# Computing v of eight token tiles by seven half-width products a pair, with its weight sums on Pool

## The chip, the cores and the metric

The kernel runs on one core of a Trainium2 chip. The metric is device time in microseconds (us) of one execution, taken as the median of several runs. One execution is profiled by the hardware; its trace lists every instruction of the five engines: TensorE (PE, with its weight loads listed apart as PEld), VectorE (DVE), ScalarE (ACT), GpSimd (Pool) and SyncE (SP, which only issues DMAs here).

## The reference

All tensors are 32-bit floats. x has 2048 rows of 512; wqkv is 512x1536, wo 512x512, w1 512x1792, w2 1792x512.

```python
xn = layernorm(x)                          # no gain or bias, eps 1e-5
q, k, v = split(xn @ wqkv)                 # 32 heads of 16
idx = pos[:, None] - arange(8) * 2         # a window of 8 keys, every second row back
logits = einsum("bhsd,bhswd->bhsw", q, k[idx]) * 16 ** -0.5    # -1e9 where idx < 0
s = einsum("bhsw,bhswd->bhsd", softmax(logits), v[idx]) @ wo
h = square(relu(xn @ w1 + b1))
out = x + s * silu(h @ w2 + b2)
```

## The kernel before

**Tiles and precision.** Rows go in 16 tiles of 128 (NT), handled in pairs of tiles a and b = a + 1. A matrix product of 32-bit floats is made of three passes over a high and a low part of each operand, (high, high), (high, low), (low, high), called PASSES. `split` makes the two parts: ACT writes the high part, DVE or Pool subtracts it to get the low part.

**Two halves of the program.** The first half loads and normalises tiles, computes q, k and v, and writes them to DRAM (`sq`, `sk`, `sv`). The second half is the MLP over chunks of 512 rows: `up` (names `ph`, in two PSUM banks with tag `h`) and `down` (`pb`), for 14 blocks f of 128 columns, with the attention's output product `pw` among them. `up` of block f ends in ACT operations on its bank: relu in place, the square rounded to `h`, and for some f (of chunk 0, f below 2 and above 11) the full square to an SBUF tile `hf`, from which Pool makes the low part; for the others the square stays in the bank and DVE (`lowh`) reads it.

**Attention.** It runs on DVE in units u of 256 rows (one pair of tiles), `pr` and `pv` being its two large products with a reduction behind each. It loads k, q and v of a unit from DRAM by DMAs that ACT's queue issues (`load_u`). Its generator `attention` is advanced by `pump`, which compares modelled clocks of PE and DVE; `defer` and `flush` put loads and exponentials at modelled times.

**q, k and v of a pair.** An ordinary product (`qkv`) of one tile and one of q, k, v is 12 matmuls of 512 columns in a bank named `pq`. Pairs 4 to 14 (SEVEN) make q and k of both tiles by a scheme of seven products instead of eight, with 6 matmuls each (`product`, banks named `pm`): the operands are quarters of the normalised tiles (`xt`), sums of them (`S`, made on DVE from `Sf`), quarters of the weights (Q0, Q1, K0, K1) and sums of these (T1 to T4), all made beforehand. The products accumulate onto each other in three banks: `sums_ps` takes Q0, T2, T3 and T4 one after the other, and each running sum is evacuated by ACT before the next product adds to it. v of these pairs is made by two ordinary products among the seven.

**Staging.** Evacuations write to staging tiles (`stg`, four buffers for k, q and v of all pairs in turn), each of which is stored by one DMA that SP issues (`store_qkv`). A buffer is reused when its store has landed.

**Order.** All engines take instructions in program order. `plan`, filled by `at(a, step, ...)`, says what stands beside which of the six steps of a pair: the transposes and splits of tiles two ahead, the sums, and by `slots` the statistics (`stats` on DVE, `spread` on ACT for tiles from 8 on: a `mean` and a `var` operation whose elementwise result is not used), `norm` and `shuffle` (four DMAs on SP, then loads of later x). `ahead` places early splits of MLP weights. Every operation goes through the helper `Ordered`, so that all of them show line 87 in the profile of before, and DMAs of `queue` line 100.

Of the kernel before, what the change touches and what calls it, by code (L numbers as in the profile page):

```python
# [30 lines left out]
GR = 8  # L31
# [17 lines left out]

STATS = 8  # L50

MATMUL, TRANSPOSE, DVE_FIXED, SHARED, SLACK, LATE, ROOM0, ROOM = 227, 150, 150, 200, 500, 3000, 500, 3500

BEHIND, FREE, LAND, LOAD = 5000, 2000, 4500, 10500

# [2 lines left out]
def body(ctx: ExitStack, tc: tile.TileContext, x, wqkv, wo, w1, b1, w2, b2, out):  # L58
# [4 lines left out]

    def price(engine, name, a, k):
        if engine == "PE":
            return MATMUL if name == "matmul" else TRANSPOSE
# [47 lines left out]
    def psH(name):  # L114
        return psum.tile([P, 512], F32, name=name, tag="h", bufs=2)
# [129 lines left out]
    def attention():  # L245
# [91 lines left out]

                defer(max(clock["V"] + FREE if u else 0, done_tiles[n][1][u] + LAND), start)

        yield from load(0, "kqv")  # L340

        for u in range(NU + 1):
            if u < NU:
                Ls[u] = att.tile([P, BI * 4, W], F32, name=f"L{u}", tag="L", bufs=2)
                for s in range(4):
                    yield from qk(u, s)
                    if u == 0 and s % 2:
                        yield from soft_a(0, s // 2)
# [12 lines left out]
            if u:  # L361
                store(u - 1)
                if u < NU - 1:
                    yield from load(u, "v")
                if u < NU:
                    yield from soft_b(u)

    stream = attention()
    coming = [None]

# [162 lines left out]
    def part_s(a, j):  # L533
        return lambda p, i: Sp[a, j // 2][:, p, j % 2, i]

    def product(ps, lhs, w, start=True):

        k = 0
        for i in range(2):
            for p, q in PASSES:  # L540
                PE.matmul(ps, lhs(p, i), wq[w][:, q, i, :], start=start and k == 0, stop=k == 5,
                          skip_group_check=True)
                k += 1

    def heads(ps):
        return ps.rearrange("p (g c) -> p g c", g=GR)

    def new_stg(t, s):
        stgs[s] = pstg.tile([P, GR, 2, CH], F32, name=f"stg{t}_{s}", tag="stg", bufs=4)

    def qkv(t, s, between=None, late=False):
# [10 lines left out]
        evacuate(t, s, ps)  # L562

    def evacuate(t, s, ps):
        if t % 2 == 0:
# [119 lines left out]
    def split_sum(w, eng):  # L685
        for i in range(2):
            split(*sum_weights[w, i], eng)

    qkv(1, 2)
    for t in range(6, 10):  # L690
        load_x(t)
# [12 lines left out]
    for a in range(2, NT, 2):  # L704
# [7 lines left out]
        if seven:  # L712
# [5 lines left out]
            at(a, n + 2 if n else n + 4, low_sums, t, 0)  # L718
            at(a, n + 3 if n else n + 5, low_sums, t, 1)
    slots = {6: ((2, 2), (2, 2), (2, 2), (2, 3)), 8: ((2, 4), (2, 5), (4, 0), (4, 1)),  # L720
             10: ((4, 4), (4, 5), (6, 0), (6, 1)), 12: ((6, 2), (6, 3), (6, 4), (6, 5)),
             14: ((8, 1), (8, 2), (8, 4), (8, 5))}
    for t, places in slots.items():
        for i, (a, step) in enumerate(places):
# [2 lines left out]
                at(a, step, shuffle, t)  # L727
    for i, w in enumerate((T2, T3, T4)):
        at(2, 1 + i, split_sum, w, G)
    for i in range(2):  # L730
        at(4, i, load_w, i)

    ahead = {(10, 2): 1, (12, 4): 1, (14, 0): 1, (14, 2): 1, (14, 4): 1}

    def beside(a, step):

        for f, args in plan.get((a, step), ()):
            f(*args)
        for n in range(ahead.get((a, step), 0)):
            next_w()  # L740
        pump(LATE)

    def pair(a):
# [13 lines left out]
    def pair_of_seven(a):  # L757

        b, last = a + 1, a + 2 == NT
        new_stg(a, 1)  # L760
        new_stg(a, 0)
        q, k = stgs[0], stgs[1]
        sums_ps, first, five = (psA(f"pm{a}_{n}") for n in range(3))
        home = dict(pool=px, tag="x", bufs=4) if last else dict(pool=hpool, tag="hf")
        u2 = home.pop("pool").tile([P, GR, CH], F32, name=f"u2_{a}", **home)
# [10 lines left out]
        A.activation(q[:, :, 0], heads(first), AF.Copy)  # L776
        beside(a, 2)

        def seventh():
            product(sums_ps, part_s(a, 2), T3, False)  # L780
            A.activation(q[:, :, 1], heads(sums_ps), AF.Copy)
            G.tensor_add(k[:, :, 1], k[:, :, 1], q[:, :, 1])
            product(five, part_s(a, 3), K1, False)
            not_before(clock["PE"])
            V.tensor_add(k[:, :, 0], u2, heads(five))
            store_qkv(b, 1)
            beside(a, 3)

        if last:
            for f in range(2):  # L790
                up(0, f)
                pump()
            lowh(0)
        qkv(b, 2, seventh)
        beside(a, 4)
        product(sums_ps, part_x(b, 1), T4, False)
        A.activation(q[:, :, 1], heads(sums_ps), AF.Copy)
        store_qkv(b, 0)
        beside(a, 5)

# [211 lines left out]
```

## Time and profile before

| | |
|---|---|
| median of 3 runs | 488.46 us (488.23 to 488.54) |
| the profiled execution: its time | 488.73 us |
| its span | 486.8 us |
| PE busy | 478.8 us, 98% of the span |
| DVE busy | 417.6 us, 86% |
| ACT busy | 235.1 us, 48% |
| Pool busy | 204.1 us, 42% |
| pair 4 starts on PE | 41.78 us |
| pair 14 starts on PE | 119.56 us |

Times in the trace count from the start of the span. A row of a timeline has start, duration, engine, source line, operation, output from input, shape and count, and in brackets the idle time before it with what ended that idle time. Matmuls are pipelined: one lasts longer than the distance to the next, so their rate is read from starts.

### The profile page before, as it was taken

How to read it: one execution, taken by the hardware profiler on the slowest of the kernel's cores; microseconds unless marked ns; L12 is line 12 of the kernel's file. 1: busy time of each engine (PE TensorE's matmuls, PEld its weight loads, DVE VectorE, ACT ScalarE, POOL GpSimd, SP SyncE). 2: the span in 40 equal slices, each digit the busy share in tenths (PEclk: the TensorE clock that was granted, in tenths of full speed). 3: DMA queues.
4: the chain of work that ended last, by engine and by line, in shares of the span. 5: the costliest groups of instructions: out<-in, count | busy, mean ns of one | idle time of the engine just before them, and what ended most of it. 6: DMA issues, size and time to landing. Idle time of an engine off the chain costs nothing.

```text
span 486.8 us, 5931 instructions
## 1 busy us (share of the span) xinstructions
PE 478.8 (98%) x2118; PEld 393.8 (81%) x2118; DVE 417.6 (86%) x348; ACT 235.1 (48%) x421; POOL 204.1 (42%) x166
## 2 busy tenths in 40 slices
PE   8999999999999999999999999999999999999996
PEld 5888788886888888888888888888888888888885
DVE  5967968986869699999999999999989999959533
ACT  5548697645575576453422444343233543423240
POOL 1347232132756699235534332653524145353210
PEclk9999999999999999999999999999999999999999
DMA  7999999898757992943708184425723852330142
GB/s 278 248 247 275 308 303 260 200 277 276 218 160 197 254 226 91 254 130 68 193 18 200 53 227 139 102 86 125 182 72 71 270 125 86 82 102 27 49 138 76
DMA packets 71002, 81.47 MB, mean 167 GB/s; under 512 B 6204, under 2 KB 55612, under 8 KB 70972
## 3 DMA queue, kind: packets, MB, share of 16 engines
q1 hardware_dynamic: 65788, 54.87, 40.8%
q10 hardware_dynamic: 5184, 26.22, 22.1%
q8 instruction: 17, 0.28, 0.3%
q14 instruction: 13, 0.11, 0.1%
HBM read 50.60 MB, written 27.32 MB: 160 GB/s over the span
## 4 chain that ended last, share of the span: by engine, by line
PE 87%; DMA 5%; DVE 4%; ACT 2%; issue 1%; SPq 0%; POOL 0%; DVEq 0%; ACTq 0%; POOLq 0%
PE pb L87 31%; PE ph L87 31%; PE pq L87 10%; PE pw L87 9%; PE pm L87 5%; DMA sk<-stg 2%; DMA sx<-xt 1%; DVE L L87 1%; DMA xb<-xn 1%; DMA x<-in_A_x 1%; DVE pxT L87 1%; SPq L100 0%; ACT stg L87 0%; DVE pr L87 0%; ACT mean L87 0%
## 5 line engine op out<-in xcount | busy, mean ns | idle before, releaser
L87 PE MATMUL pb<-w,h 128*128 128x512 f32 x672 | 160.1, 389 | 0.0
L87 PEld LDWEIGHTS pb<-w,h 128*128 128x128 f32 x672 | 126.1, 188 | 26.2
L87 POOL TENSOR_TENSOR h<-hf,h 128x512 fp32r<-128x512 f32 x46 | 72.5, 1576 | 152.0 <-ACT hf L87 152.0
L87 PE MATMUL ph<-xU,w 128*128 128x512 f32 x504 | 120.2, 389 | 0.0
L87 ACT ACTIVATE ph<-ph,b1t 128x512 f32<-128x512 f32 x56 | 37.0, 661 | 161.4 <-PE ph L87 152.7
L87 PEld LDWEIGHTS ph<-xU,w 128*128 128x128 f32 x504 | 94.6, 188 | 19.6
L87 DVE TENSOR_TENSOR pr<-k,q 128x2048 f32<-128x2048 f32 x32 | 78.9, 2466 | 4.4 <-DMA q<-sq 3.9
L87 DVE TENSOR_TENSOR pv<-v,L 128x2048 f32<-128x2048 f32 x32 | 75.4, 2355 | 6.3 <-POOL L L87 5.5
L87 DVE TENSOR_REDUCE v<-pv 128x256 f32<-128x2048 f32 x32 | 73.0, 2281 | 0.8
L87 DVE TENSOR_REDUCE L<-pr 128x128 f32<-128x2048 f32 x32 | 72.9, 2279 | 0.7
L87 PE MATMUL pw<-wot,oT 128*128 128x512 f32 (+1 forms) x204 | 45.9, 376 | 0.0
L87 PEld LDWEIGHTS pw<-wot,oT 128*128 128x128 f32 x204 | 36.8, 188 | 7.1
L87 PE MATMUL ph<-xT,w 128*128 128x512 f32 x168 | 40.0, 389 | 0.0
L87 PE MATMUL pq<-wq,xt 128*128 128x512 f32 x144 | 36.0, 392 | 1.7 <-ACT stg L87 1.7
L87 PEld LDWEIGHTS ph<-xT,w 128*128 128x128 f32 x168 | 31.5, 188 | 6.5
L87 PE MATMUL pm<-wq,S 128*128 128x512 f32 x144 | 35.9, 391 | 0.1
L87 POOL TENSOR_TENSOR w<-w1r,w 128x512 fp32r<-128x512 f32 x14 | 22.4, 1598 | 29.1 <-ACT w L87 29.1
L87 ACT ACTIVATE h<-ph 128x512 fp32r<-128x512 f32 x56 | 33.7, 602 | 1.7
L87 PEld LDWEIGHTS pq<-wq,xt 128*128 128x128 f32 x144 | 26.8, 188 | 8.3 <-ACT stg L87 2.8
L87 PEld LDWEIGHTS pm<-wq,S 128*128 128x128 f32 x144 | 26.8, 188 | 6.4 <-ACT u L87 0.7
L87 PE MATMUL pq<-wq,xT 128*128 128x512 f32 x132 | 30.9, 393 | 0.0
L87 PEld LDWEIGHTS pq<-wq,xT 128*128 128x128 f32 x132 | 24.5, 188 | 5.8 <-ACT xT L87 0.7
(82 smaller groups left out, 486.8 us busy)
## 6 DMA issues: line engine op xcount, KB each, us to landing
k<-sk ACTq DMA_DIRECT2D x8, 960.0 KB, 7.4
v<-sv ACTq DMA_DIRECT2D x8, 960.0 KB, 7.5
sx<-xt SPq DMA_DIRECT2D x12, 512.0 KB, 5.7
xU<-sx ACTq DMA_DIRECT2D x12, 512.0 KB, 7.2
x<-in_A_x SPq DMA_DIRECT2D x16, 256.0 KB, 6.3
sk<-stg SPq DMA_DIRECT2D x8, 512.0 KB, 4.3
sq<-stg SPq DMA_DIRECT2D x8, 512.0 KB, 7.3
sv<-stg SPq DMA_DIRECT2D x8, 512.0 KB, 5.0
```

The source lines that it names most:

```text
L87: return tc.keep_in_program_order(f(*a, **k))
```

## The change

v of pairs 6, 8, 10 and 12 (tiles 6 to 13, VSEVEN) is made by the seven-product scheme as well, with products 256 columns wide, since the scheme is taken here between the two column halves of v's weight. Each v product stands behind the q or k product with the same left operand. Its banks are two of tag `h` (`pv_0`, `pv_2`) and one of the four others (`pv_1`). A pair's 24 matmuls of 512 columns become 42 of 256. ACT evacuates seven results of 256 columns instead of two of 512; Pool and DVE add one sum of 256 columns each.

The four weight sums of v are made by Pool from the raw weights (`sum_v`, beside steps 1 and 5 of pair 2) and split by ACT and Pool beside steps 0 to 3 of pair 4 (`split_v`, names `vsum`). The raw weights lie in the buffer of unit 0's v, so that unit's v load, which stood in pair 2, waits until step 3 of pair 4 has been written (`v_ready`) and until the attention has come to it.

In all pairs of SEVEN the staging tiles are taken in the order k, v, q, that of their stores; before, k and q were taken at the pair's start and v at its first evacuation. A temporary `u2` is gone: the sum goes into k's staging tile. `spread` writes its unused result to SBUF instead of the `h` banks. Tile 10's and 12's places in `slots` are one or more steps later, and two entries of `ahead` move.

```diff
+VSEVEN = range(6, 14, 2)
...
-MATMUL, TRANSPOSE, ... = 227, 150, ...
+MATMUL, VMATMUL, TRANSPOSE, ... = 227, 120, 150, ...
...
-        yield from load(0, "kqv")
+        yield from load(0, "kq")
...
+                    if u == 0 and s == 1:
+                        while not v_ready:
+                            yield None
+                        yield from load(0, "v")
...
-        A.activation(psH(f"mean{t}"), xins[t], AF.Copy, scale=-1.0 / D, accum_out=means[t])
-        A.activation(psH(f"var{t}"), xins[t], AF.Square, bias=means[t], accum_out=rs[t])
+        waste = hpool.tile([P, 512], F32, name=f"waste{t}", tag="hf")
+        A.activation(waste, xins[t], AF.Copy, scale=-1.0 / D, accum_out=means[t])
+        A.activation(waste, xins[t], AF.Square, bias=means[t], accum_out=rs[t])
...
+    def sum_v(n):
+        dst, a, b = (((0, vl), (0, vr), (0, vl)), ((2, vr), (2, vr), (0, vl)), ((0, vr), (2, vr), (0, vr)),
+                     ((2, vl), (2, vl), (2, vr)))[n]
+        dst, a, b = (raws[2][:, kt:kt + 2, cols] for kt, cols in (dst, a, b))
+        G.tensor_sub(dst, a, b)
+        v_sums[n] = dst
+
+    def split_v(n):
+        i = n // 2
+        if i not in v_parts:
+            v_parts[i] = buffer(f"vsum{i}", (10, K0)[i])
+        split(*(v_parts[i][:, q, :, (vl, vr)[n % 2]] for q in range(2)), v_sums[n], G)
...
-             10: ((4, 4), (4, 5), (6, 0), (6, 1)), 12: ((6, 2), (6, 3), (6, 4), (6, 5)),
+             10: ((4, 5), (6, 0), (6, 1), (6, 2)), 12: ((6, 3), (6, 4), (6, 5), (8, 0)),
...
+    for a, step, f, n in ((2, 1, sum_v, 0), (2, 1, sum_v, 2), (2, 5, sum_v, 1), (2, 5, sum_v, 3),
+                          (4, 0, split_v, 0), (4, 1, split_v, 1), (4, 2, split_v, 2), (4, 3, split_v, 3)):
+        at(a, step, f, n)
...
-    ahead = {(10, 2): 1, (12, 4): 1, (14, 0): 1, (14, 2): 1, (14, 4): 1}
+    ahead = {(12, 3): 1, (12, 5): 1, (14, 0): 1, (14, 2): 1, (14, 4): 1}
...
+        if (a, step) == (4, 3):
+            v_ready.append(True)
         pump(LATE)
...
-        new_stg(a, 1)
-        new_stg(a, 0)
-        q, k = stgs[0], stgs[1]
+        seven = a in VSEVEN
+        for s in (1, 2, 0):
+            new_stg(a, s)
+        q, k, v = (stgs[s] for s in range(3))
...
+        if seven:
+            v_first = psA(f"pv{a}_1")
+            v_sums_ps, v_five = psH(f"pv{a}_0"), psH(f"pv{a}_2")
         product(sums_ps, part_x(a, 0), Q0)
         A.activation(first, sums_ps, AF.Copy)
+        if seven:
+            first_v()
         product(five, part_s(a, 0), T1)
         A.activation(k[:, :, 1], heads(five), AF.Copy)
+        if seven:
+            product(v_five[:, vl], part_s(a, 0), v_parts[0], cols=vl)
+            A.activation(v[:, 4:, 1], heads(v_five[:, vl]), AF.Copy)
         beside(a, 0)
-        qkv(a, 2)
-        beside(a, 1)
+        if not seven:
+            qkv(a, 2, new=False)
+            beside(a, 1)
         product(sums_ps, part_s(a, 1), T2, False)
-        A.activation(u2, heads(sums_ps), AF.Copy)
+        A.activation(k[:, :, 0], heads(sums_ps), AF.Copy)
+        if seven:
+            product(v_sums_ps[:, vl], part_s(a, 1), v_parts[0], False, vr)
+            A.activation(v[:, 4:, 0], heads(v_sums_ps[:, vl]), AF.Copy)
+            beside(a, 1)
...
+        if seven:
+            sixth()
+            product(v_sums_ps[:, vl], part_s(a, 2), v_parts[1], False, vl)
+            A.activation(v[:, :4, 1], heads(v_sums_ps[:, vl]), AF.Copy)
+            G.tensor_add(v[:, 4:, 1], v[:, 4:, 1], v[:, :4, 1])
+            beside(a, 3)
+            seventh()
+            product(v_five[:, vl], part_s(a, 3), V1, False, vr)
+            not_before(clock["PE"])
+            V.tensor_add(v[:, 4:, 0], v[:, 4:, 0], heads(v_five[:, vl]))
...
         product(sums_ps, part_x(b, 1), T4, False)
         A.activation(q[:, :, 1], heads(sums_ps), AF.Copy)
+        if seven:
+            product(v_sums_ps[:, vl], part_x(b, 1), v_parts[1], False, vr)
+            A.activation(v[:, :4, 1], heads(v_sums_ps[:, vl]), AF.Copy)
+            store_qkv(b, 2)
         store_qkv(b, 0)
         beside(a, 5)
```

The order of instructions moves at three places. First, PE in pair 6, whole before, and after as far as the twelfth of its fourteen products (`pm` are products of q and k, `pq` and `pv` of v; `wq_111`, `wq_112`, `wq_114`, `wq_117` to `wq_120` are the weight parts Q0, Q1, K1, T1 to T4, and `vsum` the sums of v). Before:

```order
L87 MATMUL pm_0_727<-wq_111,xt_611 128x512 x6
L87 MATMUL pm_2_729<-wq_117,S_0_678 128x512 x6
L87 MATMUL pq_2_753<-wq_115,xt_611 128x512 x6
L87 MATMUL pq_2_753<-wq_116,xt_611 128x512 x6
L87 MATMUL pm_0_727<-wq_118,S_0_678 128x512 x6
L87 MATMUL pm_1_728<-wq_112,xt_611 128x512 x6
L87 MATMUL pq_2_814<-wq_115,xt_614 128x512 x6
L87 MATMUL pm_0_727<-wq_119,S_1_691 128x512 x6
L87 MATMUL pm_2_729<-wq_114,S_1_691 128x512 x6
L87 MATMUL pq_2_814<-wq_116,xt_614 128x512 x6
L87 MATMUL pm_0_727<-wq_120,xt_614 128x512 x6
```

And after, PE in the same pair:

```order
L90 MATMUL pm_0_726<-wq_111,xt_613 128x512 x6
L90 MATMUL pv_0_730<-wq_115,xt_613 128x256 x6
L90 MATMUL pm_2_728<-wq_117,S_0_685 128x512 x6
L90 MATMUL pv_2_731<-vsum_590,S_0_685 128x256 x6
L90 MATMUL pm_0_726<-wq_118,S_0_685 128x512 x6
L90 MATMUL pv_0_730<-vsum_590,S_0_685 128x256 x6
L90 MATMUL pm_1_727<-wq_112,xt_613 128x512 x6
L90 MATMUL pv_1_729<-wq_116,xt_613 128x256 x6
L90 MATMUL pm_0_726<-wq_119,S_1_700 128x512 x6
L90 MATMUL pv_0_730<-vsum_653,S_1_700 128x256 x6
L90 MATMUL pm_2_728<-wq_114,S_1_700 128x512 x6
L90 MATMUL pv_2_731<-wq_116,S_1_700 128x256 x6
```

The four rows of `pq` are gone, and a row of 256 columns stands behind each row of 512; two more rows follow, T4's product and the last of v.

Second, ACT's queue around the load of unit 0's v (`v<-sv`). Before, it stood in pair 2, between splits of weights (`wq<-wqraw`) and evacuations:

```order
L87 ACTIVATE wq_118<-wqraw_2_129 128x512
L87 ACTIVATE wq_118<-wqraw_3_131 128x512
L87 DMA v_428<-sv 128x1x1920
L87 ACTIVATE stg_1_443<-pq_1_430 128x8x64
L87 ACTIVATE wq_119<-wqraw_0_123 128x512
```

After, ACT issues it in pair 6, behind `norm` of tile 11 (`xn_794`, its second row):

```order
L90 ACTIVATE Sf_792<-pxT_764 128x256
L90 ACTIVATE xn_794<-x_496,shift_714,rs_713 128x4x4x32
L90 ACTIVATE stg_0_725<-pm_1_727 128x8x64
L90 ACTIVATE stg_2_724<-pv_1_729 128x4x64
L90 ACTIVATE xn_794<-x_498,shift_768,rs_767 128x4x4x32
L90 DMA v_827<-sv 128x1x1920
L90 ACTIVATE stg_0_725<-pm_0_726 128x8x64
L90 ACTIVATE stg_2_724<-pv_0_730 128x4x64
```

The load has moved from pair 2 to pair 6, and stands between evacuations of pair 6 (`stg_0` is q, `stg_2` is v).

Third, PE in chunk 0 of the MLP, the products `up` of f = 12 and f = 13, with the engines that they wait for. Before:

```order
L87 MATMUL ph0_12_1935<-xT0_168,w12_1822 128x512 [waits DVE_49]
L87 MATMUL ph0_12_1935<-xT0_168,w12_1822 128x512
L87 MATMUL ph0_12_1935<-xT0_168,w12_1822 128x512 [waits Pool_49]
L87 MATMUL ph0_12_1935<-xT0_168,w12_1822 128x512 x9
L87 MATMUL ph0_13_1955<-xT0_168,w13_1864 128x512 [waits DVE_49]
L87 MATMUL ph0_13_1955<-xT0_168,w13_1864 128x512
L87 MATMUL ph0_13_1955<-xT0_168,w13_1864 128x512 [waits Pool_49]
L87 MATMUL ph0_13_1955<-xT0_168,w13_1864 128x512 x9
```

After:

```order
L90 MATMUL ph0_12_2038<-xT0_168,w12_1925 128x512 [waits DVE_49]
L90 MATMUL ph0_12_2038<-xT0_168,w12_1925 128x512
L90 MATMUL ph0_12_2038<-xT0_168,w12_1925 128x512 [waits Pool_49]
L90 MATMUL ph0_12_2038<-xT0_168,w12_1925 128x512 x9
L90 MATMUL ph0_13_2058<-xT0_168,w13_1970 128x512 [waits PE_49,Activation_49]
L90 MATMUL ph0_13_2058<-xT0_168,w13_1970 128x512
L90 MATMUL ph0_13_2058<-xT0_168,w13_1970 128x512 [waits Pool_49]
L90 MATMUL ph0_13_2058<-xT0_168,w13_1970 128x512 x9
```

`ph0_13` lay in the other bank than `ph0_12` before, and waited for DVE, the last reader of `ph0_11`; now it lies in the bank of `ph0_12` and waits for ACT, the last reader of that.

More of the change, by code (lines that the diff above doesn't have):

```diff
@@ L50 @@
 STATS = 8
[L52 removed]
+MATMUL, VMATMUL, TRANSPOSE, DVE_FIXED, SHARED, SLACK, LATE, ROOM0, ROOM = 227, 120, 150, 150, 200, 500, 3000, 500, 3500
 BEHIND, FREE, LAND, LOAD = 5000, 2000, 4500, 10500
@@ L65, in price @@
         if engine == "PE":
-            return MATMUL if name == "matmul" else TRANSPOSE
+            if name != "matmul":
+                return TRANSPOSE
+            return MATMUL if a[0].shape[-1] != 256 else VMATMUL
         ap = k["in_"] if name == "tensor_reduce" else k.get("out", a[0] if a else None)
@@ L534, in part_s, with product @@
         return lambda p, i: Sp[a, j // 2][:, p, j % 2, i]
-    def product(ps, lhs, w, start=True):
+    def product(ps, lhs, w, start=True, cols=slice(0, 512)):
         k = 0
+        w = wq[w] if isinstance(w, int) else w
         for i in range(2):
             for p, q in PASSES:
-                PE.matmul(ps, lhs(p, i), wq[w][:, q, i, :], start=start and k == 0, stop=k == 5,
+                PE.matmul(ps, lhs(p, i), w[:, q, i, cols], start=start and k == 0, stop=k == 5,
                           skip_group_check=True)
@@ L545, in heads, with qkv @@
     def heads(ps):
-        return ps.rearrange("p (g c) -> p g c", g=GR)
+        return ps.rearrange("p (g c) -> p g c", c=CH)
     def new_stg(t, s):
         stgs[s] = pstg.tile([P, GR, 2, CH], F32, name=f"stg{t}_{s}", tag="stg", bufs=4)
-    def qkv(t, s, between=None, late=False):
+    def qkv(t, s, between=None, late=False, new=True):
         ps = psA(f"pq{t}_{s}")
@@ L561, in qkv, with evacuate @@
                 between()
-        evacuate(t, s, ps)
-    def evacuate(t, s, ps):
-        if t % 2 == 0:
+        evacuate(t, s, ps, new)
+    def evacuate(t, s, ps, new=True):
+        if t % 2 == 0 and new:
             new_stg(t, s)
@@ L782, in seventh, with both @@
             G.tensor_add(k[:, :, 1], k[:, :, 1], q[:, :, 1])
+        def seventh():
             product(five, part_s(a, 3), K1, False)
             not_before(clock["PE"])
-            V.tensor_add(k[:, :, 0], u2, heads(five))
+            V.tensor_add(k[:, :, 0], k[:, :, 0], heads(five))
             store_qkv(b, 1)
+        def both():
+            sixth()
+            seventh()
             beside(a, 3)
[L789 to L794, printed above, removed]
+        if seven:
+            sixth()
+            product(v_sums_ps[:, vl], part_s(a, 2), v_parts[1], False, vl)
+            A.activation(v[:, :4, 1], heads(v_sums_ps[:, vl]), AF.Copy)
+            G.tensor_add(v[:, 4:, 1], v[:, 4:, 1], v[:, :4, 1])
+            beside(a, 3)
+            seventh()
+            product(v_five[:, vl], part_s(a, 3), V1, False, vr)
+            not_before(clock["PE"])
+            V.tensor_add(v[:, 4:, 0], v[:, 4:, 0], heads(v_five[:, vl]))
+        else:
+            if last:
+                for f in range(2):
+                    up(0, f)
+                    pump()
+                lowh(0)
+            qkv(b, 2, both)
         beside(a, 4)
```

13 lines of the change are left out of this document (10 added, 3 removed).

## The prediction

> **What bounds the kernel now.** I read the page's busy times and chain first, then PE stage by stage, then the waits inside the stage that is changed.
>
> ```profile
> PE 478.8 (98%) x2118; PEld 393.8 (81%) x2118; DVE 417.6 (86%) x348; ACT 235.1 (48%) x421; POOL 204.1 (42%) x166
> PE 87%; DMA 5%; DVE 4%; ACT 2%; issue 1%; SPq 0%; POOL 0%; DVEq 0%; ACTq 0%; POOLq 0%
> ```
>
> TensorE (PE) works for 98% of the span and carries 87% of the chain that ends last. So time is won by fewer PE columns or by taking away PE's stalls, and lost by a new PE stall. The view by windows, cut at the first matmul of pairs 4, 6, 8, 10, 12 and 14, gives per stretch the length and then the busy time of PE, PEld, DVE, ACT and POOL, the clock, the DMA share and GB/s:
>
> ```profile
> 41.78:56.88 15.10, 15.10 (x67) 12.26 (x66) 12.99 (x16) 10.58 (x23) 8.09 (x9) 1.00 1.10 309
> 56.88:72.80 15.92, 15.32 (x67) 12.31 (x66) 11.16 (x19) 15.07 (x35) 5.09 (x13) 1.00 1.10 295
> 72.80:87.87 15.07, 15.07 (x67) 12.31 (x66) 12.68 (x15) 11.08 (x25) 4.81 (x8) 1.00 0.81 219
> 87.87:102.83 14.96, 14.96 (x67) 12.39 (x66) 12.74 (x20) 9.47 (x18) 4.67 (x3) 1.00 1.10 266
> 102.83:119.56 16.73, 15.58 (x67) 12.23 (x66) 12.54 (x15) 6.89 (x14) 1.29 (x1) 1.00 0.94 270
> ```
>
> The clock is full. A pair is 66 matmuls of 512 columns. What one takes in a stream is read from two neighbours in PE's timeline, start to start:
>
> ```profile
> 105.55 2.88 PE L87 MATMUL pq<-wq,xt 128*128 128x512 f32 x12
> 108.27 1.52 PE L87 MATMUL pm<-wq,S 128*128 128x512 f32 x6
> 112.22 1.66 PE L87 MATMUL pq<-wq,xt 128*128 128x512 f32 x6 [1.07 <-ACT stg L87]
> ```
>
> Twelve take 108.27 − 105.55 = 2.72 us, so one takes 0.2267 and a pair 66 × 0.2267 = 14.96. The five pairs exceed this by 0.14, 0.96, 0.11, 0 and 1.77 us: 2.98 us of stall, nearly all in pairs 6 and 12. In pair 12, PE waits for ACT's evacuation (`stg`), and ACT for a store out of the staging buffer that it must reuse:
>
> ```profile
> 111.57 0.60 ACT L87 ACTIVATE stg<-pq 128x512 f32<-128x512 f32 x1 [5.22 <-DMA sk<-stg]
> ```
>
> ```profile
> 102.17 0.37 SPq L100 DMA_DIRECT2D sk<-stg x1
> ```
>
> This `sk` store landed 9.4 us after its issue. Pair 6's stall is of the other kind: ACT, busy 15.07 of 15.92 us, comes late with the accumulators.
>
> **Columns.** The last 36 matmuls of the kernel are 12 of 512 and 24 of 256 columns:
>
> ```profile
> 477.24 5.75 PE L87 MATMUL pw<-wot,oT 128*128 128x512 f32 x36
> ```
>
> ```profile
> L87 PEld LDWEIGHTS pw<-wot,oT 128*128 128x128 f32 x204 | 36.8, 188 | 7.1
> ```
>
> 5.75 − 2.72 leaves 3.03 us for 24 narrow ones with the pipeline's tail (389 − 227 ns of a 512); without it 0.120 each. Each of the four pairs loses 24 × 0.2267 = 5.44 us and gains 42 × 0.120 = 5.04: −0.40, together **−1.60 us**. [...] The rows show 120 and 227, so I keep −1.60.
>
> **Old stalls.** The accumulators `pq` on which both large waits stood are gone in pairs 6 to 12, and k's staging buffer is now claimed in sending order. I take all **−2.98 us** out here and price what is late next by itself.
>
> **The new pair.** A product and its v half take 6 × 0.2267 + 6 × 0.120 = 2.08 us, seven of them 14.56. ACT gets seven evacuations of 256 columns instead of two of 512. Its durations, start to start:
>
> ```profile
> 56.73 0.63 ACT L87 ACTIVATE S<-Sf 128x512 fp32r<-128x512 f32 x1 [3.13 <-DVE Sf L87]
> 57.27 0.58 ACT L87 ACTIVATE stg<-pq 128x512 f32<-128x512 f32 x1
> ...
> 65.78 0.84 ACT L87 ACTIVATE xn<-x,shift,rs 128x512 f32<-128x512 f32 x1
> 66.48 0.61 ACT L87 ACTIVATE u<-pm 128x512 f32<-128x512 f32 x1
> ...
> 78.44 0.60 ACT L87 ACTIVATE stg<-pq 128x512 f32<-128x512 f32 x1 [2.12 <-PE pq L87]
> 78.94 1.08 ACT L87 ACTIVATE xt<-pxT 128x512 fp32r<-128x512 f32 x2
> 79.89 0.40 ACT L87 ACTIVATE Sf<-pxT 128x256 f32<-128x256 f32 x1
> 80.16 0.63 ACT L87 ACTIVATE mean<-x 128x512 f32<-128x512 f32 x1
> ...
> 81.65 0.58 ACT L87 ACTIVATE u<-pm 128x512 f32<-128x512 f32 x1
> ```
>
> S costs 0.54, a 512 evacuation 0.50, `xn` 0.70, two `xt` 0.95, a 256 evacuation 0.27, a `spread` (mean and var) 1.49.
>
> *Pair 6* starts at 56.88, and 2.08 us later, at 58.96, its T1 product needs the bank that the evacuation of pair 4's T4 product frees. ACT reaches S at 56.73, held by DVE; then follow the new weight split (0.50), `stg` of v (0.50), S (0.54) and the T4 evacuation (0.58): 56.73 + 0.54 + 0.50 + 0.50 + 0.54 + 0.58 = 59.39. PE waits about **0.5**; the spread that stood in this queue has moved behind.
>
> *Pair 8* starts at 56.88 + 0.5 + 14.56 = 71.94. Its first v evacuation goes into the buffer that pair 6's k store empties, and is due after the first two products with their v halves, at 71.94 + 2 × 2.08 = 76.10. The rows for it:
>
> ```profile
> 71.50 0.38 SPq L100 DMA_DIRECT2D sk<-stg x1
> ```
>
> ```profile
> v<-sv ACTq DMA_DIRECT2D x8, 960.0 KB, 7.5
> sk<-stg SPq DMA_DIRECT2D x8, 512.0 KB, 4.3
> ```
>
> ```profile
> 66.00:74.00 8.00, 8.00 (x37) 6.61 (x36) 4.40 (x9) 7.80 (x18) 3.49 (x7) 1.00 1.08 277
> ```
>
> ```profile
> 32.86 0.52 ACTq L87 DMA_DIRECT2D v<-sv x1
> ```
>
> K1's product is earlier than before, but the shuffle of tiles 10 and 11, now a step later, stands ahead on SP's queue, so I leave the issue at 71.5. Unit 0's v load has moved from 32.86 to behind `xn` of tile 11, at about 67.5: 960 KB more in a stretch that already shows a DMA share of 1.08. At 277 GB/s it is 3.5 us of everybody's queue, so the store lands at L = 71.5 + 4.3 + 3.5 = 79.3. From L, ACT must do v 0.27, xn 0.70, k 0.50, v 0.27, xt 0.95, Sf 0.27, spread 1.49, q 0.50, v 0.27, spread 1.49, and T3's evacuation 0.60: 7.31 us, for a T4 product due at 71.94 + 6 × 2.08 = 84.42. PE's loss is therefore L − 77.1, here **2.2 us**; it ranges from 0 (no share taken: L = 75.8) to 3.8 (the 9.4 us of pair 12's row: L = 80.9).
>
> *Pairs 10 to 14*: the same wait can come back in pair 12, but no spreads stand in ACT's queue there, and with a landing as late as before (9.4 us) my count leaves 1.1 us of stall. I take **0.3** of 0 to 1.1. New stalls together: 0.5 + 2.2 + 0.3 = **3.0 us**, bounds 0.5 and 5.4 (called S below).
>
> **The MLP's banks.** The two `h` banks now come out of phase: `ph0_12` and `ph0_13`, multiplied back to back, share one bank. The trace before:
>
> ```profile
> 194.36 5.60 PE L87 MATMUL ph<-xT,w 128*128 128x512 f32 x24
> 199.80 5.60 PE L87 MATMUL pb<-w,h 128*128 128x512 f32 x24
> ```
>
> ```profile
> 198.47 0.59 ACT L87 ACTIVATE hf<-ph 128x512 f32<-128x512 f32 x1
> ```
>
> `ph0_13` would start at 194.36 + 2.72 = 197.08; it must now wait until ACT has read `ph0_12` the third time, 198.47 + 0.59 = 199.06, plus some 0.05. That is **+2.03 us**. Nothing covers it: 24 `pb` matmuls are queued behind it on PE. Before this place PE runs on without a gap, so neither this nor an earlier start is given back.
>
> **Free.** Pool's new subtractions and splits: two of the former stand before `rs` of tiles 6 and 7.
>
> ```profile
> 34.88 0.55 POOL L87 TENSOR_TENSOR rs<-rs,mhalf 128x1 f32<-128x1 f32 x1
> 38.12 0.79 POOL L87 TENSOR_TENSOR rs<-rs,mhalf 128x1 f32<-128x1 f32 x1 [2.68 <-DVE rs L87]
> 38.88 5.69 POOL L87 TENSOR_TENSOR wq<-wqraw,wq 128x512 fp32r<-128x512 f32 x4
> ```
>
> Four of 512 columns take 5.69, so two 2.85: they fit in front of 38.12. If that cover failed, norms of tiles 6 and 7 would come up to 2.85 us late, 18 us ahead of pair 6. Moving unit 0's v load costs attention nothing, since its first use is late:
>
> ```profile
> L87 DVE TENSOR_TENSOR pv<-v,L x32: 2281/2293/3102, 96.2 to 451.7; 128x2048 f32<-128x2048 f32 x32
> ```
>
> The added Pool and DVE sums of v (256 columns) lie behind the products that PE runs on, and nobody but the `sv` store waits for them.
>
> **Sum.** −1.60 − 2.98 + 3.0 + 2.03 = +0.45 us on the profiled 488.73 us, which is 0.27 above the median 488.46: median **488.9 us**. A difference from no change can be told here from about 0.2%, 0.98 us.
>
> **Rivals.** *The store lands in time* (L under 77.9, 6.4 us after its issue or less). For it: the median of `sk` stores is 4.3 us and the moved load may fall into a thinner moment. With L = 77.1 or less, only 0.5 + 0.3 of new stall is left: −1.60 − 2.98 + 0.8 + 2.03 = −1.75, median 486.7. Faster. Chance 0.31.
>
> *The store lands late, and the wait of pair 12 comes back* (L above 79.8, 8.3 us after issue). For it: the 9.4 us row; loads and stores queue through the whole stage (DMA share about 1). With L = 80.9 and 1.1 in pair 12, S = 5.4: +2.85, median 491.3. Slower. Chance 0.32. From L = 79.8 on, the sum is over 0.98.
>
> *Weight loads set the pace of narrow matmuls.* A load takes 188 ns, longer than 120. If each of the 168 narrow matmuls took 0.188, columns cost 168 × 0.188 − 96 × 0.2267 = +9.8 us; with PE slower, ACT's new stalls go, and −2.98 + 2.03 + 9.8 gives 497.3. The 24 narrow matmuls at 0.120 speak against it. [...] Chance 0.04.
>
> **Numbers.** The forecast (L from 77.9 to 79.8, the sum within 1 us of before, a median of 487.5 to 489.4) has 0.33, little more than each neighbour, since a landing is the least certain number here: the rows for one store run from 4.3 to 9.4 us. Of its 0.33, I give 0.01 to a faster and 0.04 to a slower time, for the smaller bounds (old stalls that stay in part, pair 12's 1.1). That makes faster 0.31 + 0.01 = 0.32, same 0.28, slower 0.32 + 0.04 + 0.04 = 0.40. The range runs from S = 0.5 (−2.05: 486.4) to the late rival (491.3); what lies outside is the weight-load rival and the ends of the two others.
>
> **What would show it.** Right: pairs 6 to 12 at 14.56 us and narrow matmuls at 0.12; `ph` of f = 13 idle about 2 us behind ACT `hf`; an idle of about 2 us in pair 8 behind ACT `stg`, with ACT waiting for DMA `sk`. Wrong: no wait in pair 8 (then faster), a wait of over a microsecond in pair 12 as well (then slower), or no gap before `ph0_13`.

## The result and the profile after

The changed kernel takes 492.35 us in the median (491.94 to 493.87, six executions) against 488.50 of the kernel before in the same comparison: a ratio of 1.0081, with a 95% interval of 1.0060 to 1.0102. It is slower by 3.85 us, where 488.9 with 486.4 to 491.3 was forecast. The profiled execution took 493.87 us, with a span of 491.6. The page of the changed kernel, busy times and granted clock:

```profile
PE 480.8 (98%) x2190; PEld 397.8 (81%) x2190; DVE 426.2 (87%) x352; ACT 239.8 (49%) x441; POOL 223.7 (46%) x178
PEclk9999999999999999899999999999999999999999
```

PE is still 98% busy, but one of the 40 slices has a lower clock (8 tenths for 9), which no slice had before. The view by windows of the changed kernel, cut at the first matmul of pairs 4, 6, 8, 10, 12 and 14, and then around `ph0_13` (columns as in the prediction, PEclk third from the end):

```profile
41.92:57.45 15.53, 15.45 (x67) 12.21 (x66) 13.55 (x17) 12.10 (x26) 14.28 (x14) 1.00 1.04 270
57.45:72.51 15.06, 14.94 (x85) 12.94 (x84) 14.89 (x20) 14.93 (x37) 8.66 (x11) 1.00 0.99 274
72.51:90.66 18.15, 15.21 (x86) 13.01 (x85) 14.24 (x17) 13.28 (x32) 6.35 (x15) 1.00 0.92 234
90.66:105.50 14.84, 14.84 (x86) 12.91 (x85) 14.19 (x22) 9.16 (x20) 2.85 (x3) 1.00 1.03 251
105.50:120.34 14.84, 14.84 (x86) 12.91 (x85) 14.11 (x19) 8.77 (x20) 4.08 (x3) 1.00 0.87 277
195.21:199.96 4.75, 2.88 (x14) 2.07 (x12) 4.75 (x4) 2.78 (x5) 0.23 (x1) 1.00 0.18 41
199.96:204.40 4.44, 4.44 (x12) 3.50 (x13) 4.37 (x3) 0.00 (x0) 1.28 (x1) 0.62 0.00 0
```

Pairs 6, 10 and 12 are shorter than before (15.92, 14.96, 16.73), pair 8 is 3.08 us longer. The last window holds twelve matmuls of 512 columns: 2.72 us at full clock, here 4.44 at a granted clock of 0.62. PE's timeline of the changed kernel shows three idle times, each with the engine that ended it:

```profile
82.78 1.66 PE L90 MATMUL pm<-wq,S 128*128 128x512 f32 x6 [1.71 <-ACT stg L90]
...
88.46 1.65 PE L90 MATMUL pm<-wq,xt 128*128 128x512 f32 x6 [1.23 <-ACT stg L90]
...
199.96 4.61 PE L90 MATMUL ph<-xT,w 128*128 128x512 f32 x12 [1.87 <-ACT hf L90]
204.40 5.61 PE L90 MATMUL pb<-w,h 128*128 128x512 f32 x24
```

Against the trace before, PE is 0.57 us late where pair 6 starts (57.45 for 56.88). Pairs 6 to 12 together take 62.89 us for 62.68, +0.21; pair 14 adds 0.07. The bank wait adds 2.03 (199.96 against 195.21 + 2.72 = 197.93; the view's 1.87 counts from the modelled end of the last matmul before it), and the twelve matmuls behind it, at the low clock, 4.44 − 2.72 = 1.72. The sum is 4.60, and the last group of matmuls indeed starts 4.61 later (481.85 for 477.24).

Pair 8's wait, in ACT's and SP's timelines of the changed kernel:

```profile
81.16 0.38 ACT L90 ACTIVATE stg<-pv 128x256 f32<-128x256 f32 x1 [4.29 <-PE pv L90]
```

```profile
71.12 2.20 SPq L103 DMA_DIRECT2D x<-in_A_x x2
73.42 1.11 SPq L103 DMA_DIRECT2D sk<-stg x1
```

```profile
66.42 0.53 ACTq L90 DMA_DIRECT2D v<-sv x1
```

At 81.16, ACT starts the first evacuation of pair 8's v into its staging buffer. The view names PE, which had long been done (the product started at 76.00, and six narrow matmuls take 0.71); what came then is the store from the buffer, issued at 73.42. The view of this one store gives its time to landing, 7.6 us, so it landed at 81.0:

```profile
L103 SPq DMA_DIRECT2D sk<-stg x1: 1111/1111/1111, 73.4 to 73.4; - x1
DMA to landing us min/median/max: 7.6/7.6/7.6
```

### The profile page after: what moved, and what is told of

Read it like the earlier page. It is cut to its first block, busy times and chain, and to the rows that moved or that the text cites. A ratio compares the mean times of both kernels' runs of the same rounds, so it can differ in the third digit from the quotient of the medians.

```text
span 491.6 us, 6119 instructions
## 1 busy us (share of the span) xinstructions
PE 480.8 (98%) x2190; PEld 397.8 (81%) x2190; DVE 426.2 (87%) x352; ACT 239.8 (49%) x441; POOL 223.7 (46%) x178
## 4 chain that ended last, share of the span: by engine, by line
PE 86%; DMA 5%; ACT 3%; DVE 2%; issue 2%; POOL 1%; SPq 0%; POOLq 0%; ACTq 0%; DVEq 0%
PE ph L90 31%; PE pb L90 31%; PE pw L90 9%; PE pm L90 8%; PE pq L90 4%; DMA x<-in_A_x 2%; PE pv L90 2%; DMA sq<-stg 2%; DMA sk<-stg 2%; ACT stg L90 1%; ACT waste L90 1%; POOL stg L90 1%; POOL rs L90 1%; DVE Sf L90 0%; DVE xn L90 0%
## 5 line engine op out<-in xcount | busy, mean ns | idle before, releaser
L90 POOL TENSOR_TENSOR h<-hf,h 128x512 fp32r<-128x512 f32 x46 | 67.0, 1456 | 165.7 <-ACT hf L90 161.1
L90 DVE TENSOR_TENSOR pv<-v,L 128x2048 f32<-128x2048 f32 x32 | 78.8, 2461 | 3.8 <-POOL L L90 3.1
L90 PE MATMUL ph<-xT,w 128*128 128x512 f32 x168 | 41.9, 401 | 1.9 <-ACT hf L90 1.9
L90 PEld LDWEIGHTS ph<-xT,w 128*128 128x128 f32 x168 | 32.6, 195 | 9.2 <-ACT hf L90 2.3
L90 PE MATMUL pm<-wq,S 128*128 128x512 f32 x144 | 37.3, 395 | 1.9 <-ACT stg L90 1.7
L90 PEld LDWEIGHTS pm<-wq,S 128*128 128x128 f32 x144 | 25.8, 188 | 7.6 <-ACT stg L90 2.2
L90 POOL TENSOR_TENSOR w<-w1r,w 128x512 fp32r<-128x512 f32 x14 | 26.3, 1881 | 10.7 <-ACT w L90 10.7
L90 PE MATMUL pm<-wq,xt 128*128 128x512 f32 x108 | 27.8, 394 | 1.2 <-ACT stg L90 1.2
L90 ACT ACTIVATE hf<-ph 128x512 f32<-128x512 f32 x46 | 27.3, 594 | 0.6 <-POOL h L90 0.6
```

The costliest lines, as they stand in the source:

```text
L90: return tc.keep_in_program_order(f(*a, **k))
```

## The experiments

Eight kernels derive from the changed one and four from the kernel before. Each is compared with the kernel before on its own chip.

**The banks in turn.** The `h` banks are taken in turn.

```diff
-        return psum.tile([P, 512], F32, name=name, tag="h", bufs=2)
+        turn[0] += 1
+        return psum.tile([P, 512], F32, name=name, tag=f"h{turn[0] % 2}", bufs=1)
...
+            turn[0] += a % 4 == 0
             v_sums_ps, v_five = psH(f"pv{a}_0"), psH(f"pv{a}_2")
+            turn[0] += a % 4 == 0
```

> The changed kernel, with only the two h banks kept in turn, so that ph0_13 lies in the other bank than ph0_12. Theory (the bank wait cost 2.03 us of idle, and the lower clock behind it is a consequence of that idle): PE goes on without a gap at ph0_13 at a granted clock of 1.00, the profiled span is up to 3.75 us shorter than the changed kernel's 491.6, and the median about 489.7, 2 to 3.7 us under 492.35. Rival (the low clock is a matter of the single run and not of the idle): a stretch at a clock near 0.6 shows again somewhere, and only 2 us are won.

Median 490.84 us, ratio 1.0064 (1.0041 to 1.0087). PE's timeline of this kernel, in pair 8 and at `ph0_13`:

```profile
84.43 1.64 PE L90 MATMUL pm<-wq,S 128*128 128x512 f32 x6 [1.92 <-ACT stg L90]
85.91 1.45 PE L90 MATMUL pv<-vsum,S 128*128 128x256 f32 x6
87.15 2.57 PE L90 MATMUL pm<-wq,S 128*128 128x512 f32 x6
89.56 0.88 PE L90 MATMUL pv<-wq,S 128*128 128x256 f32 x6
...
199.91 3.03 PE L90 MATMUL ph<-xT,w 128*128 128x512 f32 x12 [0.44 <-DVE h L90]
```

The wait of 1.87 is gone; 0.44 us of another, for DVE, is left. The low clock now stands in pair 8, behind an idle of 1.92 us and one product: six narrow matmuls take 1.24 us instead of 0.71, at a granted clock of 0.51, and six wide ones 2.41 instead of some 1.4, at 0.54. So in these two profiles it comes behind a long idle (1.87 and 1.92 us) and not with `ph0_13`, whose twelve matmuls take 2.87 us here. In 5 of 11 executions the mean clock is 0.996 or less. The span is only 1.5 us shorter than that of the changed kernel, because the low clock came again and pair 6 starts 1.34 us later in this profile (58.79 for 57.45).

**The bank wait alone**, in the kernel before.

```diff
-        return psum.tile([P, 512], F32, name=name, tag="h", bufs=2)
+        turn[0] += name == "ph0_13"
+        turn[0] += 1
+        return psum.tile([P, 512], F32, name=name, tag=f"h{turn[0] % 2}", bufs=1)
```

> The kernel before, with only ph0_13 forced into the bank of ph0_12. Theory: the idle of 2.0 us appears behind ACT hf, and in some executions the clock falls behind it, so that the median is 2.0 to 3.8 us above before, 490.5 to 492.3. Rival (low clock belongs to something else in the changed kernel): 2.0 us and never more, 490.5, at a mean clock of 0.999.

Median 491.61 us, ratio 1.0067 (1.0042 to 1.0093). Six of twelve executions have a mean clock of 0.996, with times from 491.84 to 494.64; the six others have 0.998 or more and lie between 488.70 and 491.38. The idle is the same as in the changed kernel. PE's timeline in an execution without the low clock:

```profile
197.52 3.03 PE L87 MATMUL ph<-xT,w 128*128 128x512 f32 x12 [1.87 <-ACT hf L87]
```

The twelve matmuls behind it take 2.87 us, start to start, against 2.72 in a stream and 4.44 at the clock of 0.62. So the wait alone costs 2.03 us up to their start (197.52 against 192.77 + 2.72), and 2.18 with them. Of the executions that were not profiled only the time and the mean clock are known: the six with the lower clock lie 2.5 us above the others in the median. A mean clock 0.003 to 0.004 lower over 488 us is an estimated 1.5 to 2 us of this, which fits the 4.44 − 2.87 = 1.57 that the low clock took in the changed kernel; the rest is not explained.

**A shorter and a longer idle**, both in the kernel with the bank wait alone. The first reads the bank twice instead of three times, the second four times.

```diff
-        A.activation(h[:, 0], ph, AF.Square)
...
-        A.activation(full, ph, AF.Square)
+        first = (c, f) == (0, 12)
+        if first:
+            A.activation(full, ph, AF.Square)
+        A.activation(h[:, 0], full if first else ph, AF.Copy if first else AF.Square)
+        if not first:
+            A.activation(full, ph, AF.Square)
```

```diff
         A.activation(full, ph, AF.Square)
+        if (c, f) == (0, 12):
+            A.activation(full, ph, AF.Square)
```

> The kernel before with ph0_13 in the bank of ph0_12, but ACT reads that bank only twice after its product (the full square first, then the rounded high part from SBUF), so that PE's idle is some 1.4 us instead of 1.87. [...]

> The same with one more read of the bank by ACT (the full square written twice), so that PE's idle is some 2.4 us. Theory: the clock falls in more executions than the half seen with 1.87 us, and the median is 2.6 + 1.7 = 4.3 us above before. Rival (the fall is a matter of chance, not of the length): half of the executions again, and two groups at 2.6 and 4.3 us above before.

PE's timelines, of the shorter and of the longer one:

```profile
196.76 3.02 PE L87 MATMUL ph<-xT,w 128*128 128x512 f32 x12 [1.43 <-ACT hf L87]
```

```profile
198.56 3.06 PE L87 MATMUL ph<-xT,w 128*128 128x512 f32 x12 [2.50 <-ACT hf L87]
```

With 1.43 us of idle, none of 12 executions has a mean clock under 0.999; the median is 490.12, ratio 1.0032 (1.0011 to 1.0053). With 2.50 us, 3 of 6 have 0.996 or less (493.57 to 495.14 us, the others 490.28 to 492.07); median 492.82, ratio 1.0092 (1.0055 to 1.0129). So the length matters: none of 12 at 1.43 us, six of 12 at 1.87. That the clock always holds at 1.43 is not shown, nor is a limit between the two; and three of six at 2.50 are too few to say whether the share rises. The idle times are those of the profiled executions, which here had no low clock.

**Unit 0's v load later**, beside step 3 of pair 8, with the banks in turn.

```diff
+        def load_v0():
+            tiles["v", 0] = load_u("v", 0)
+            landing["v", 0] = clock["PE"] + LOAD
...
-                        yield from load(0, "v")
...
-        if (a, step) == (4, 3):
-            v_ready.append(True)
+        if (a, step) == (8, 3):
+            v_load[0]()
```

> The changed kernel with the banks in turn, and with unit 0's v load issued by ACT beside step 3 of pair 8 instead of in pair 6. Theory (the moved load delays pair 6's k store, which landed 7.7 us after its issue): the store lands within about 5 us of its issue, pair 8's two waits shrink from 2.94 us to under 0.7, and the median is 2 to 3 us below that of the run with banks alone, about 487. Rival (the store is late because it is issued late, at 73.4 us, behind the shuffle and x loads on SP, and lands in a crowd anyway): the waits stay above 2 us, and the median stays within 1 us of the other run.

SP's timeline and ACT's of this kernel:

```profile
71.03 1.08 SPq L103 DMA_DIRECT2D x<-in_A_x x2
72.22 0.38 SPq L103 DMA_DIRECT2D sk<-stg x1
```

```profile
76.94 0.39 ACT L90 ACTIVATE stg<-pv 128x256 f32<-128x256 f32 x1 [0.16 <-PE pv L90]
...
157.81 0.54 ACTq L90 DMA_DIRECT2D q<-sq x1
158.39 0.63 ACT L90 ACTIVATE L<-L 128x512 f32<-128x512 f32 x1 [8.36 <-DMA w2r<-in_B_w]
```

The view of this store, too, gives its time to landing:

```profile
L103 SPq DMA_DIRECT2D sk<-stg x1: 378/378/378, 72.2 to 72.2; - x1
DMA to landing us min/median/max: 4.6/4.6/4.6
```

The x loads in front are issued in 1.08 us instead of 2.20, the store 1.2 us earlier, and it has landed after 4.6 us, when ACT wants the buffer at 76.94. Both waits of pair 8 are gone (it takes 14.84 us), as the theory has it. The median of 490.08 (ratio 1.0037, 1.0010 to 1.0064) is yet only 0.8 below the banks alone, as the rival has it, since other waits came up: ACT stands 8.4 us before the q load of unit 2, PE waits twice for DVE's `h` (0.78 and 0.99 us), and three times for ACT (0.63 us in pair 6, 0.50 in pair 12, 0.43 in pair 14). Why that load was held so long is not settled.

**Tile 10's shuffle a step earlier**, the load left in pair 6, banks in turn.

```diff
-             10: ((4, 5), (6, 0), (6, 1), (6, 2)), 12: ((6, 3), (6, 4), (6, 5), (8, 0)),
+             10: ((4, 4), (4, 5), (6, 0), (6, 1)), 12: ((6, 3), (6, 4), (6, 5), (8, 0)),
```

> The changed kernel with the banks in turn, with tile 10's places as before, so that the shuffle and the x loads leave SP a step earlier, while unit 0's v load stays in pair 6. Theory (the moved load is what delays pair 6's k store): the store is issued about 1 to 2 us earlier than at 73.4 us but still takes over 6 us to land, and pair 8 keeps a wait of 1 us or more. Rival (the late issue behind shuffle and x loads is enough): pair 8's waits go as they did with the later v load.

Median 491.33 us, ratio 1.0073 (1.0048 to 1.0098). SP's timeline and ACT's:

```profile
71.66 0.50 SPq L103 DMA_DIRECT2D sk<-stg x1
```

```profile
67.06 0.53 ACTq L90 DMA_DIRECT2D v<-sv x1
...
81.69 0.38 ACT L90 ACTIVATE stg<-pv 128x256 f32<-128x256 f32 x1 [4.16 <-DMA sk<-stg]
```

The store leaves 1.8 us earlier than in the changed kernel and lands 10 us after its issue, at nearly the same time as there. PE still idles 1.46 and 1.21 us in pair 8. The landing goes with the load's issue, not with the store's: in all four kernels with the load in pair 6 (the changed one, this one, the banks alone and the grouped one below) the store lands 14.6 to 14.8 us after the load's issue, though its own issue comes 4.6 us behind the load here and 6.9 to 7.0 in the others. (1.57 us of idle came in pair 6, where a spread again stood ahead of the T4 evacuation.)

**The early weight splits alone**, in the kernel before.

```diff
-    ahead = {(10, 2): 1, (12, 4): 1, (14, 0): 1, (14, 2): 1, (14, 4): 1}
+    ahead = {(12, 3): 1, (12, 5): 1, (14, 0): 1, (14, 2): 1, (14, 4): 1}
```

> The kernel before, with only the two early splits of MLP weights moved, from steps (10,2) and (12,4) to (12,3) and (12,5), as the change has them. Theory (pair 12's stall of 1.77 us went because the weight loads no longer run ahead of pair 10's k store): the stall in pair 12 goes or falls below 0.4 us, and the median falls by about 1.4 to 1.8 us, to 486.9. Rival (it went because the accumulator pq is gone and v's evacuation is due later): the stall stays, and the time is that of before.

Median 486.86 us against 487.88, ratio 0.9981 (0.9964 to 0.9998). Its profile has no wait of PE in pair 12 (PE is busy for all of the 16.40 us from 102.6 to 119.0). But neither have the profiles of the three kernels with the bank wait alone, whose code is that of before up to the MLP: in four profiles of this stage, PE's wait is there once. What is in all four is a late store: pair 10's k store lands 7.6 to 9.3 us after its issue, and ACT waits for it until 109.7 to 111.6. With the splits moved it leaves 0.6 to 1.1 us earlier and lands after 7.1 us, and ACT, which takes that evacuation at 108.7, no longer waits for it. Of the kernel before, 16 of 34 executions on that chip took over 488.3 us, of this one 2 of 12. The splits make PE's wait rarer, which the counts suggest rather than prove.

**Narrow products in groups**: in steps 0 to 3, two wide products, then their two narrow ones; the last step as it was. Banks in turn, the v load in pair 8.

```diff
         product(sums_ps, part_x(a, 0), Q0)
         A.activation(first, sums_ps, AF.Copy)
-        if seven:
-            first_v()
         product(five, part_s(a, 0), T1)
         A.activation(k[:, :, 1], heads(five), AF.Copy)
         if seven:
+            first_v()
             product(v_five[:, vl], part_s(a, 0), v_parts[0], cols=vl)
```

> The changed kernel with the banks in turn and unit 0's v load in pair 8, and with the narrow products of v grouped: two or so wide products, then their narrow ones, so that a pair of tiles changes from narrow to wide matmuls four times instead of seven. Theory (the wide matmuls that follow a narrow run come 0.01 us apart too slowly, 0.04 to 0.05 us for six): an undisturbed pair takes about 14.70 us instead of 14.84. Rival (the narrow ones or all wide ones are slower by a fixed amount each): 14.84 us again. The time of the whole says little here, since other waits differ.

Pair 10 starts at 88.38 and pair 12 at 103.05 in PE's timeline of this kernel, where the changed kernel's timeline shows the rate of a wide product (90.66 to 92.07) and a narrow one (92.07 to 92.78):

```profile
88.38 1.56 PE L90 MATMUL pm<-wq,xt 128*128 128x512 f32 x6
...
103.05 1.55 PE L90 MATMUL pm<-wq,xt 128*128 128x512 f32 x6
```

```profile
90.66 1.56 PE L90 MATMUL pm<-wq,xt 128*128 128x512 f32 x6
92.07 0.88 PE L90 MATMUL pv<-wq,xt 128*128 128x256 f32 x6
92.78 1.56 PE L90 MATMUL pm<-wq,S 128*128 128x512 f32 x6
```

Six narrow matmuls take 0.71, 0.118 each, as forecast. Six wide ones behind a narrow run take 1.41 instead of 1.36. Grouped, pair 10 takes 14.67 us. Not all of the 0.17 to 14.84 is the grouping's, though: in pairs 6 and 8 of the changed kernel a product and its half follow each other by 2.10 instead of 2.12 (wide ones 1.39), and in the kernel with only the banks in turn, pairs 10 and 12 take 14.70 us each without any grouping:

```profile
92.37 1.55 PE L90 MATMUL pm<-wq,xt 128*128 128x512 f32 x6
...
107.07 1.55 PE L90 MATMUL pm<-wq,xt 128*128 128x512 f32 x6
...
121.77 1.55 PE L90 MATMUL pm<-wq,xt 128*128 128x512 f32 x6
```

So a pair of alternating products goes at one of two paces, 14.70 or 14.84 us, and in these profiles changes between them only at a break in the stream; what sets the pace is not shown. Grouping is worth 0.03 to 0.17 us a pair. The median is 486.80 against 488.27, ratio 0.9967 (0.9946 to 0.9987): faster than the kernel before, and by its ratio than the changed kernel, which ran on another chip. Here pair 6's k store landed after 6.1 us, and pair 8 idles 0.73 us.

**The grouped kernel with the load in pair 6**, which separates the two edits.

> The grouped kernel (banks in turn, narrow products in groups), but with unit 0's v load in pair 6 as the change has it. Theory (the moved load in pair 6 costs pair 8's wait, whatever the order of the products): pair 6's k store lands 7 us or more after its issue, pair 8 idles 2 us or more in all, and the median is 2 to 4 us above that of the grouped kernel with the later load, about 489.5. Rival (grouping itself removed the wait, since v's evacuations come later in it): waits as with the later load, about 487.

Median 489.98, ratio 1.0063 (1.0041 to 1.0085). SP's, ACT's and PE's timelines:

```profile
72.40 0.75 SPq L103 DMA_DIRECT2D sk<-stg x1
```

```profile
80.39 0.38 ACT L90 ACTIVATE stg<-pv 128x256 f32<-128x256 f32 x1 [4.46 <-DMA sk<-stg]
```

```profile
82.01 3.03 PE L90 MATMUL pm<-wq,S 128*128 128x512 f32 x12 [1.91 <-ACT stg L90]
85.47 0.98 PE L90 MATMUL pv<-vsum,S 128*128 128x256 f32 x6 [0.43 <-ACT stg L90]
87.68 1.65 PE L90 MATMUL pm<-wq,xt 128*128 128x512 f32 x6 [0.52 <-ACT stg L90]
```

It landed 7.9 us after its issue, with 2.86 us of idle in pair 8: the load alone brings the wait back. Over all profiles, this store takes 7.6, 7.8, 7.9 and 10.0 us to land with the load in pair 6, and 3.6 to 6.1 us in the ten kernels that have it in pair 2 or pair 8.

**The grouped kernel with ordinary v products everywhere** (`VSEVEN = ()`); the sums of v's weights are still made, and not used.

> The grouped kernel with its v of tiles 6 to 13 made by ordinary products again; sums of v's weights, the later v load, the slots and the early weight splits stay as they are there. Theory (in groups, a pair with seven narrow products takes 14.67 us against 14.96): some 1.2 us of columns are lost for four pairs, less what the grouped kernel waits in pairs 6 and 8 (0.9 us in its profile), so the two are within about 1 us, this one the slower, 487.2. Rival (the gain of the grouped kernel comes from the moved weight splits alone, and narrow products are worth nothing): this one is as fast or faster, 486.8 or less.

Median 486.48 against 487.11, ratio 0.9987 (0.9974 to 1.0001), with no idle of PE named in its profiled stage. The two theories are not separated by the times: the medians come from two chips, and the ratios to before, 0.9967 grouped and 0.9987 here, have intervals that overlap. In the profiles the rival is nearer: pairs 6 to 12 take 60.74 us grouped and 60.40 here, so what four pairs save in groups, 4 × 0.29 = 1.16 us, goes back in pairs 6, 8 and 12. What the grouped kernel has over before would then come from the rest of the change.

**Narrow products in pairs 10 and 12 only** (`VSEVEN = range(10, 14, 2)` in the grouped kernel), and **the rest of the change without narrow products, sums or a later load**, on one chip.

> The grouped kernel with seven narrow products only in pairs 10 and 12, which idled nowhere in the grouped kernel; v of pairs 6 and 8 by ordinary products. Theory (an undisturbed pair gains 0.29 us in groups, and what the four pairs lose again lies in pairs 6 and 8): 0.58 us under the kernel without narrow products, about 486.0, with pairs of 14.67 us in 10 and 12 and no wait. Rival (narrow products bring waits wherever they are, through ACT's seven evacuations): a new wait of 0.3 us or more in pair 10, 12 or 14, and the time is that of the kernel without them or above.

> The kernel before with only what the change has beside the narrow products: slots, early weight splits, spread to SBUF, staging taken at the pair's start; no sums of v's weights, unit 0's v load in pair 2 as before. Theory (the gain of the grouped kernels over before comes from here): no wait in pairs 6 to 12, 0.5 to 1.5 us under before, about 486.4, as the kernel with the unused sums (486.48). Rival (the later v load is needed for it): a wait in pair 6 or 8 remains, and the time is that of before.

With two pairs: 485.73 against 488.25, ratio 0.9957 (0.9942 to 0.9973), the lowest ratio here. Its span is 483.7, and pair 12 starts and ends in PE's timeline at

```profile
101.80 1.55 PE L90 MATMUL pm<-wq,xt 128*128 128x512 f32 x6
...
116.44 1.55 PE L90 MATMUL pm<-wq,xt 128*128 128x512 f32 x6
```

14.64 us, with no wait in either pair. Without narrow products: 487.38, ratio 0.9986 (0.9969 to 1.0002), with one wait of 0.44 us in pair 6. The two kernels' medians stand 1.65 us apart, more than the 0.64 of columns that two pairs save against 14.96; the later load and the 0.44 are in the difference too, so how much of it is the narrow products' is not shown.

## Why the prediction failed

The median lies 1.05 us above the end of the range. The clock alone does not account for that: the three executions with a mean clock of 0.997 or more took 491.94 to 492.12 us, which is above the range too. Three terms of the sum were too good (columns, pair 8, and what stands ahead of pair 6), and one cost was not in it (the clock).

**Columns, −1.60: mis-sized.** The narrow matmul was priced right, 0.118 for 0.120. What failed is the step "A product and its v half take 6 × 0.2267 + 6 × 0.120 = 2.08 us": behind a narrow run six wide matmuls take 1.39 to 1.41 us instead of 1.36, so that a product and its half take 2.10 in pairs 6 and 8 and 2.12 in pairs 10 and 12. Seven of them are 14.70 and 14.84 us, not 14.56. The four pairs save 0.52 + 0.24 = 0.76 us instead of 1.60. A row of narrow matmuls at the end of a stream could not show this.

**The bank wait, +2.03: right, and not the whole price.** The idle came out to the hundredth. "Nothing covers it" missed that an idle can cost beyond itself: in the profiled execution the clock fell to 0.62 for 4.44 us, and the twelve matmuls there took 1.72 us longer than in a stream (0.15 longer behind the same idle at a full clock). In three of the six executions of the changed kernel the mean clock is 0.996 or less, so the median carries only a part of it. The kernel with the bank wait alone shows as much, with a mean clock of 0.996 in 6 of 12 executions behind 1.87 us of idle; with the idle at 1.43 us, none of 12 is under 0.999.

**Pair 8, +2.2: right mechanism, too small.** The store landed at 81.0 instead of 79.3. Its 7.6 us from issue to landing are near the forecast's 4.3 + 3.5 = 7.8, and the 3.6 to 6.1 us of the ten kernels without the load there fit both parts. What failed is "I leave the issue at 71.5": it came 1.9 us later. The x loads ahead of it on SP began at 71.12 instead of 69.22 and took 2.20 us to issue instead of 1.08, which used up the 1.2 us that had lain between them and the store. With pair 8's start 0.57 later, L − 77.7 is 3.5, taking for L the 81.16 at which ACT goes on; measured are 18.15 − 14.70 = 3.45. This passes the threshold of the second rival (L above 79.8), of which the other half, pair 12's wait, did not come.

**Old stalls, −2.98: gone in this profile but for pair 4's 0.14, and not a saving to count on.** Pair 12's 1.77 us stand in one of four profiles of the old stage, so a saving of that size could not be counted on for the median; that the profiled execution was one with this wait was luck. Nor did the order of taking staging tiles end the wait for the store: in pair 12 of the changed kernel, ACT still waits for pair 10's `sk`, 1.75 us until 111.57. PE was not held by it: it is busy for all 14.84 us of pair 12.

**What held.** Narrow matmuls are not paced by their weight loads: they start 0.118 us apart, with loads of 0.188, and in pair 10 of the changed kernel 12.91 us of loads lie beside 14.84 us of busy PE. Pair 6's wait was 0.29 of 0.5: after `pv` at 58.81 + 0.71, the next product came at 59.81. Pool's new sums were covered, as forecast: they end at 37.57, and `rs` of tile 7 waits for DVE until 38.65.

The 0.57 us ahead of pair 6 was not forecast. The trace shows 0.14 of it at the start of pair 4 and 0.39 in pair 4's second product, which takes 1.75 us (43.29 to 45.04) instead of 1.36 because its operand `S` is late. The chain to `S` begins with the statistics of tile 7, for whose x DVE waited until 37.47 instead of 36.94. In the grouped kernels with two such pairs and with none, which make the same sums, this product takes its usual 1.36 us; why x landed later is not shown.

Put together, the forecast's +0.45 misses 0.84 on columns, 1.25 in pair 8, 1.72 behind the bank wait at the low clock, 0.57 ahead of pair 6 with the 0.14 of pair 4 that stayed, and 0.07 in pair 14; 0.14 in pair 6 and 0.3 in pairs 10 to 14 came out better. That makes the 4.60 measured in the profiled execution.

## What to carry to other kernels

Look for the load that a change moves, and ask whose store it now travels with: here 960 KB moved into a crowded stretch (a DMA share of 1.08 before) cost some 3 us in pair 8, more than the 0.76 us that the narrow products of four pairs saved. Price an edit of a matmul's shape in the stream in which it will stand, with its neighbours, not by a uniform run elsewhere. A wait in a single profile may belong to that execution: before its removal is counted as a gain, it should be seen in a second one.

## What the runs showed of the hardware

With an idle of PE of 1.87 us, the mean clock was 0.996 in 6 of 12 executions, and with 2.50 us 0.995 or 0.996 in 3 of 6; with 1.43 us it was 0.999 or more in all 12. Length is not all: the grouped kernel with the load in pair 6 idles 1.91 us in its profile, and none of its six executions has a mean clock under 0.997. Where the fall was profiled behind 1.87 us, twelve matmuls took 4.44 us at a granted clock of 0.62, against 2.87 behind the same idle without it and 2.72 in a stream.

Narrow matmuls of 256 columns run at 0.118 us each, beside weight loads of 0.188; six wide ones behind a run of them take 1.38 to 1.41 us in the changed kernel, where PE does not wait, instead of 1.36 (1.5 to 4% more).

Pair 6's store of 512 KB landed 7.6 to 10.0 us after its issue with a load of 960 KB issued 4.6 to 7.0 us ahead of it, and 3.6 to 6.1 without that load. A late landing was also seen without such a load: pair 10's store took 7.6 to 9.3 us in the kernel before and the three with its code.
